# A value product in eleven passes instead of twelve, with the low half of the probabilities written in two pieces

## The chip, the cores and the metric

The kernel runs on one core of one Trainium2 chip. The metric is the device time of one execution in microseconds; the median of three runs of the kernel before is 1019.92 us (1019.78 to 1021.08). The engines are named as in the profile: PE (TensorE matmuls), PEld (weight loads), DVE (VectorE), ACT (ScalarE), POOL (GpSimd) and SP (the engine whose queue issues most of the DMAs).

## The reference

Attention over 8 batches and 12 heads of 448 tokens and 64 channels, followed by a gated feed-forward stage with token mixing:

```python
q_n, k_n = rmsnorm(q, g_q), rmsnorm(k, g_k)
attn = softmax(q_n @ k_n.T / sqrt(64))
x = attn @ v                               # back to (8, 448, 768)
x_prev = x shifted by one token
xk = mu_k * x + (1 - mu_k) * x_prev        # xr likewise with mu_r
k = relu(xk @ w_k)                         # 768 -> 1024
out = sigmoid(xr @ w_r) * ((k * k) @ w_v)  # 1024 -> 768
```

## The kernel before

**Number format.** Inputs are f32, and PE multiplies f16. An f32 value is therefore held as a sum hi + lo of two f16 numbers, and a product of two such values is made of three f16 products: hi·hi, hi·lo and lo·hi. The first batch (quads 0 to 2, pairs 0 to 5) is done in f32 instead.

**Tiling of the attention.** Two heads are a pair (48 pairs, six to a batch) and two pairs a quad (24 quads). The keys of a head are 448 = 3.5 chunks of 128. `scores` makes, for 128 queries and both heads of a pair, two score tiles `sc` of 128x448 in PSUM; there are seven such groups in a quad. `expo` takes the row maximum (DVE) and the exponential (ACT). `probs` computes the reciprocal of the row sum, and `split` writes the normalized probabilities into a tile `nat` of the ring of that name (a borrowed buffer of it is called `natx` in the trace): ACT writes hi as f16, then one DVE instruction writes lo = value − hi, 448 wide. When both heads are split, one DMA transpose on SP's queue turns `nat` into the tile `pT`, so that keys lie on partitions. From quad 3 on there are 21 quads x 7 groups x 2 heads = 294 such splits.

**Value product.** `attends` multiplies, for each pair, `pT` by the values (`vh` and `vl`, hi and lo f16). Flat in `nat` stand hi of head 0, hi of head 1, lo of head 0, lo of head 1, so 14 chunks of 128. Chunk 3 is half head 0 and half head 1, and the value layout prepared on the host has zeros in the half that is not meant. The product takes 4 chunks of hi by `vh` and by `vl`, and 4 chunks of lo by `vh`: the 12 passes of `PASSES`. A pass is two matmuls, one for each head, side by side in the two column halves of the array; each streams 448 columns. The result goes into the PSUM tile `ot`, and ACT copies it into an `x` tile.

**Feed-forward.** For each batch, `mix` blends x and x_prev into `xk` (for `w_k`) and `xr` (for `w_r`): POOL, then DVE (the instruction that writes `df` or `dfx`), then ACT (hi) and POOL (lo). `moe` then runs on PE: the key product of a batch (`mm<-xk,wkh` in the trace, 144 matmuls), which needs all six `xk`, and then the output products (`mm<-wrh,xr` and `mm<-wvh,kk`, 252 or 336 matmuls). The weights too are scaled and split on the chip during the first batches; the first output product waits for the last weight tile.

**Order.** A planner (`Plan`) runs when the kernel is built. Every step above is a thread that yields instructions; the planner keeps a clock for each engine, prices each instruction (`price`) and repeatedly emits the one that could start first, less a priority. The order it finds is fixed for each engine, and an engine runs its instructions in that order: one that waits holds back all that stands behind it. For a DVE instruction of n elements with two tensor inputs the price is n/0.96 + 128 ns above 64 elements, and n/0.96 + 64 ns up to 64. Priorities put the `xk` mixes forward while `moe` wants them; the feed-forward matmuls fill PE between the attention's steps.

Of the kernel before, what the change touches and what calls it, by code (L numbers as in the profile page):

```python
# [12 lines left out]
AF = mybir.ActivationFunctionType  # L13
ALU = mybir.AluOpType
# [3 lines left out]
HD = 64  # L18
NT = 7
S = NT * HD  # L20
# [57 lines left out]
U32 = 3  # L78
# [42 lines left out]
def whole(ap):  # L121
    c = ap.shape[-1]
    return ap.rearrange("p a c -> p (a c)").bitcast(F32).rearrange("p (a c) -> p a c", c=c)
# [297 lines left out]
def attn_moe_kernel(tc, q, k, v, g_q, g_k, mu_k, mu_r, w_k, w_v, w_r, out):  # L421
# [13 lines left out]
    T, V, A, G_, SP = (Engine(n, e) for n, e in (("PE", nc.tensor), ("DVE", nc.vector), ("ACT", nc.scalar), ("POOL", nc.gpsimd), ("SP", nc.sync)))  # L435
# [23 lines left out]
    NQ, NPAIR, NSS, NSL = len(quads), len(pairs), 4 * NT, (NT + 1) // 2  # L459
# [10 lines left out]
    def until(f):  # L470
        while not f():
            yield f
# [33 lines left out]
    for name, plan_ in (("kk", KK_LENT), ("xk", XK_LENT)):  # L506
# [4 lines left out]
        o = 0  # L511
        for n in plan_:
            r = R[n]
# [172 lines left out]
    def vfree(i, vf):  # L686
        FR[i] = FR.get(i, 0) + 1
        if FR[i] == 2:
            VFREE.append(vf)
# [66 lines left out]
    def scores():  # L756
        for gi, (u, x, t0) in enumerate(groups):
# [31 lines left out]
            for j in range(2):  # L789
                plan.spawn(expo(gi, j, both, sums, D, tp), PRIO_E)  # L790
            plan.spawn(probs(gi, both, sums, D, tp), PRIO_E)

    def expo(gi, j, both, sums, D, tp):
# [11 lines left out]
    def probs(gi, both, sums, D, tp):  # L805
        u, x, t0 = groups[gi]
        yield from until(lambda: len(D) == 2 and st["g"] == gi)
        for i in (2 * u, 2 * u + 1) if t0 == NT - 1 else (2 * u + x,):
            if i not in PT:
                yield from until(lambda: PTFREE[i % 2] and (i != 2 * U32 or PTFREE[1]))  # L810
                PTFREE[i % 2] = False
                PT[i] = (whole(PTQ[:, :, :]) if u < U32 else PTQ)[:, :, i % 2 * S:(i % 2 + 1) * S]
                CNT[i] = 0
        if tp is not None:
            st["g"] += 1
            yield from probs_pe(u, x, t0, sums, tp)
            return
        tp = yield from R["nat"].get(u < 3)
        ph = tp.rearrange("p a c -> p (a c)").rearrange("p (a c) -> p a c", c=S)
        st["g"] += 1  # L820
        r = sums[:, 8:11:2]
        yield V.tensor_scalar(out=r, in0=both[0][:, S:S + 2], scalar1=1e-9, scalar2=2.0 ** -15, op0=ALU.add, op1=ALU.mult)
        yield V.reciprocal(out=r, in_=r)
        E = {}
        for j in range(2):
            plan.spawn(split(j, both[j], r, ph, E), PRIO_P)
        yield from until(lambda: len(E) == 2)
        phf = ph.rearrange("p a c -> p (a c)")
        if t0 < NT - 1:
            yield SP.dma_start_transpose(out=PT[2 * u + x][:, :, (t0 + x) * HD:(t0 + x + 2) * HD], in_=phf)  # L830
            CNT[2 * u + x] += 1
        else:
            yield SP.dma_start_transpose(out=PTQ[:, :, S - HD:S + HD], in_=phf)
            CNT[2 * u] += 1
            CNT[2 * u + 1] += 1
        R["nat"].put(tp)

    def probs_pe(u, x, t0, sums, tp):
        r = sums[:, 8:11:2]
        yield V.tensor_scalar(out=r, in0=sums[:, 4:7:2], scalar1=1e-9, scalar2=2.0 ** -15, op0=ALU.add, op1=ALU.mult)  # L840
        yield V.reciprocal(out=r, in_=r)
        tf = tp.bitcast(F32).rearrange("p a c -> p (a c)")
        for j in range(2):
            w = tf[:, j * S:(j + 1) * S]
            yield G_.tensor_scalar(out=w, in0=w, scalar1=r[:, j:j + 1], scalar2=0.0, op0=ALU.mult, op1=ALU.add)
        c0 = S - HD if t0 == NT - 1 else x * S + (t0 + x) * HD
        for a0 in range(0, NT, 4):
            m = min(4, NT - a0)
            st["zq"] += 1
            z = yield from banks["sc"].get()  # L850
            st["zq"] -= 1
            yield [T.transpose(form=("tr", TR_COST * m), out=z[:, a * P:(a + 1) * P], in_=tf[:, (a0 + a) * P:(a0 + a + 1) * P], identity=ident) for a in range(m)]
            src = z[:, 0:m * P].rearrange("p (a c) -> p a c", c=P)
            if u < U32:
                dst = whole(PTQ[:, :, :])[:, a0:a0 + m, c0:c0 + P]
                yield A.copy(out=dst, in_=src) if plan.pick("ACT", "DVE") == "ACT" else V.tensor_copy(out=dst, in_=src)
            else:
                hi, lo = (PTQ[:, h + a0:h + a0 + m, c0:c0 + P] for h in (0, NT))
                yield A.copy(out=hi, in_=src)
                yield V.tensor_tensor(out=lo, in0=src, in1=hi, op=ALU.subtract)  # L860
            banks["sc"].put(z)
        R["nat"].put(tp)
        for i in (2 * u, 2 * u + 1) if t0 == NT - 1 else (2 * u + x,):
            CNT[i] += 1

    def split(j, sp, r, ph, E):
        yield A.activation(out=ph[:, j], in_=sp[:, 0:S], func=AF.Copy, scale=r[:, j:j + 1])
        yield V.scalar_tensor_tensor(out=ph[:, 2 + j], in0=sp[:, 0:S], scalar=r[:, j:j + 1], in1=ph[:, j], op0=ALU.mult, op1=ALU.subtract)
        E[j] = True
        banks["sc"].put(sp)  # L870

    PASSES = [p for c in range(NSL) for p in ((0, 0, c), (0, 1, c))] + [(1, 0, c) for c in range(NSL)]

    def attends():
        for i in range(NPAIR):
            yield from until(lambda: CNT.get(i) == 4 and i in VV)
            x = yield from R["x"].get()
            vh, vl, iv = VV.pop(i)
            pT = PT.pop(i)
            av = yield from banks["ot"].get()  # L880
            ops = []
            passes = [(0, 0, c) for c in range(NSL)] if vl is None else PASSES
            for j, (pl, hl, c) in enumerate(passes):
                for h in range(2):
                    ops.append(T.matmul(
                        form=("av", len(passes) * (4 if vl is None else 1) * S / 2.368),
                        out=av[h * HD:(h + 1) * HD, 0:S],
                        lhsT=(vl if hl else vh)[:, NSL * h + c, :],
                        rhs=pT[:, NT * pl + (NSL - 1) * h + c, :],
                        start=(j == 0), stop=(j == len(passes) - 1)))  # L890
            yield ops
            PTFREE[i % 2] = True
            if vl is None:
                vfree(i, vh)
            else:
                R["vh"].put(vh)
                R["vl"].put(vl)
            for lo, hi in ((0, NT),) if i % 2 == 0 else ((NT - 1, NT), (0, NT - 1)):
                o = 0 if i % 2 == 0 or lo else HD
                yield A.activation(out=x[:, 1 + lo:1 + hi, :].rearrange("p t c -> p (t c)"), in_=av[:, o:o + (hi - lo) * HD], func=AF.Copy, scale=1.0 if iv is None else iv)  # L900
            banks["ot"].put(av)
            yield G_.memset(out=x[:, 0, 0:1], value=0.0)
            yield G_.tensor_copy(out=x[:, 0, 1:HD], in_=x[:, NT, 0:HD - 1])
            XT[i] = [x, 2]
# [247 lines left out]
def layouts(inputs):  # L1152
    import numpy as np

    q, k, v = (np.asarray(inputs[n]) for n in ("q", "k", "v"))
    b, h = q.shape[:2]
    nq = b * h // 4

    def tokens(a):
        return a.reshape(b, h, HD, NT, HD)  # L1160

    def quads(a):
        a = tokens(a).reshape(nq, 2, 2, HD, NT, HD)
        return np.ascontiguousarray(a.transpose(0, 1, 3, 2, 4, 5)).reshape(nq, P, 2 * S)

    qd, kd = quads(q), quads(k)
    a = tokens(q).reshape(nq, 4, HD, NT, HD)[PE_T:]
    pair = a[:, :, :, :NT - 1].reshape(-1, 4, HD, NT // 2, 2, HD).transpose(0, 4, 2, 3, 1, 5).reshape(-1, P, (NT - 1) * 2 * HD)
    last = a[:, :, :, NT - 1].reshape(-1, 2, 2, HD, HD).transpose(0, 1, 3, 2, 4).reshape(-1, P, 2 * HD)
    qd[PE_T:] = np.concatenate([pair, last], axis=2)  # L1170
    a = tokens(v).reshape(b * h // 2, 2, HD, NT, HD)
    n = (NT + 1) // 2
    vd = np.zeros((b * h // 2, 2, HD, 2 * n, HD), v.dtype)
    for x in range(2):
        for e in range(2):
            t = (x + e) % 2
            o = n * x + (x and not e)
            c = (NT + 1 - t) // 2
            vd[:, e, :, o:o + c] = a[:, x, :, t::2]
    return {"q": qd, "k": kd, "v": vd.reshape(b * h // 2, P, 2 * n * HD)}  # L1180


# [30 lines left out]
```

## Time and profile before

| | |
|---|---|
| median of three runs | 1019.92 us |
| the profiled execution | 1018.41 us, of which its span is 1016.6 us |
| busy over the span | PE 923.4 us (91%), DVE 790.2 (78%), ACT 744.7 (73%), POOL 691.1 (68%) |
| matmuls of the value product, pairs 6 to 47 | 672 with `vh`, 336 with `vl` |
| DVE instructions that write lo of the probabilities | 244 into `nat` and 50 into `natx`, mean 674 ns |

PE's share of 91% is an average over a start in which it waits and a long stretch in which it hardly does, so the stages have to be read apart. The granted clock of PE is 0.97 on average; it is lower only in the first 235 us and in the last two.

### The profile page before, as it was taken

Reading aid. Unit: us, or ns where it says so; the run is one execution under the profiler, and the core shown is the slowest. Engines: PE = TensorE matmul, PEld = TensorE weight load, DVE = VectorE, ACT = ScalarE, POOL = GpSimd, SP = SyncE. Lnnn points to the kernel's source line nnn. Section 1 sums busy time; section 2 is a strip of 40 time slices with the busy share of each in tenths; the row PEclk is TensorE's granted clock in tenths of the full one; section 3 lists DMA queues with packets and bytes.
Section 4 is the critical chain, followed back from the end, with each engine's and each line's share of the span. In section 5 each row is a group of like instructions: output and inputs, shape, how many; then the busy total and the mean of one; then the engine's idle time right before and its main releaser. Section 6 shows DMA issues by size and latency. Waiting matters only on the chain. (4 is left out here: it accounts for less than half of the span.)

```text
span 1016.6 us, 18482 instructions
## 1 busy us (share of the span) xinstructions
PE 923.4 (91%) x6166; PEld 486.1 (48%) x6166; DVE 790.2 (78%) x1969; ACT 744.7 (73%) x1753; POOL 691.1 (68%) x734
## 2 busy tenths in 40 slices
PE   1577868859999999999999999999998999999998
PEld 1343434434544555445544555455444554455564
DVE  5797979978999798979996898799887998753000
ACT  3576858978698889888987888988896898842311
POOL 2687879841789577968787659965886567556501
PEclk9798969978999999999999999999999999999999
DMA  7323358776794998698858968877877897440000
GB/s 244 111 91 89 103 150 167 168 180 120 179 189 106 203 203 183 144 191 191 174 131 170 195 144 198 186 155 163 173 139 168 195 188 163 103 78 32 1 33 31
DMA packets 371134, 148.14 MB, mean 146 GB/s; under 512 B 338272, under 2 KB 355168, under 8 KB 371040
## 3 DMA queue, kind: packets, MB, share of 16 engines
q1 hardware_dynamic: 351792, 129.20, 57.9%
q10 hardware_dynamic: 19248, 17.77, 5.9%
q8 instruction: 48, 0.79, 0.3%
q14 instruction: 46, 0.38, 0.1%
HBM read 51.98 MB, written 11.01 MB: 62 GB/s over the span
## 5 line engine op out<-in xcount | busy, mean ns | idle before, releaser
L272 PE MATMUL mm<-wvh,kk 128*128 128x384 f16 x896 | 234.1, 326 | 3.4 <-POOL kk L272 3.0
L272 ACT ACTIVATE sc<-sc,sums 128x448 f32<-128x448 f32 x294 | 181.3, 620 | 41.7 <-DVE sums L272 38.5
L272 PE MATMUL mm<-xk,wkh 128*128 128x448 f16 x768 | 208.3, 353 | 3.7 <-DVE bstat L272 1.8
L272 DVE TENSOR_REDUCE sums<-sc 128x1 f32<-128x448 f32 x336 | 193.0, 612 | 11.6 <-PE sc L272 11.0
L272 ACT ACTIVATE nat<-sc,sums 128x448 f16<-128x448 f32 (+1 forms) x274 | 166.8, 652 | 20.9 <-DVE sums L272 7.2
L272 PE MATMUL mm<-wrh,xr 128*128 128x384 f16 x672 | 177.3, 328 | 0.0
L272 PEld LDWEIGHTS <-kk 128*128 128x128 f16 (+1 forms) x1362 | 129.6, 98 | 99.5 <-issue 14.9
L272 DVE SCALAR_TENSOR_TENSOR nat<-sc,sums,nat 128x448 f16<-128x448 f32 x244 | 159.6, 674 | 19.9 <-ACT nat L272 19.3
L272 PE MATMUL mm<-wvl,kk 128*128 128x384 f16 x448 | 146.0, 326 | 0.0
L272 PE MATMUL sc<-stk 64*128 64x448 f16 (+3 forms) x1104 | 129.1, 378 | 11.7 <-DVE nat L272 7.8
L272 PE MATMUL mm<-xk,wkl 128*128 128x448 f16 x384 | 135.3, 352 | 0.0
L272 PEld LDWEIGHTS <-xr 128*128 128x128 f16 x1008 | 96.1, 98 | 72.5 <-issue 12.5
L272 PE MATMUL mm<-wrl,xr 128*128 128x384 f16 x336 | 110.0, 327 | 0.0
L272 PEld LDWEIGHTS <-wkh 128*128 128x128 f16 x768 | 72.0, 98 | 78.6 <-issue 17.4
L272 PE MATMUL ot<-pT,vh 128*64 128x448 f16 x672 | 100.9, 359 | 5.4 <-DMA pT<-nat 5.4
L272 DVE SCALAR_TENSOR_TENSOR o<-o,mm 128x384 f32<-128x384 f32 x56 | 30.5, 545 | 90.4 <-PE mm L272 60.1
L272 POOL TENSOR_TENSOR qk<-qk,ss 128x896 f32<-128x896 f32 x36 | 62.9, 1749 | 42.6 <-DVE ss L272 19.2
L272 POOL TENSOR_TENSOR o<-o,bsc 128x384 f32<-128x384 f32 x48 | 42.8, 891 | 61.0 <-DVE o L272 48.7
L272 ACT ACTIVATE o<-mm,bsc 128x128 f32<-128x128 f32 x144 | 44.3, 386 | 49.5 <-PE mm L272 37.4
L272 DVE SCALAR_TENSOR_TENSOR df<-x,bsc,df 128x448 f32<-128x448 f32 x68 | 66.5, 993 | 4.2 <-POOL df L272 4.0
L272 POOL TENSOR_TENSOR nat<-qk,nat 128x896 f16<-128x896 f32 x29 | 56.3, 1940 | 19.3 <-ACT nat L272 19.1
L272 POOL TENSOR_TENSOR nat<-nat 128x448 f32<-128x448 f32 x38 | 45.0, 1184 | 34.8 <-ACT nat L272 15.8
(166 smaller groups left out, 1782.2 us busy)
## 6 DMA issues: line engine op xcount, KB each, us to landing
vf<-in_v_dram SPq DMA_DIRECT2D x48, 256.0 KB, 3.1
out_dram<-o SPq DMA_DIRECT2D x28, 384.0 KB, 2.8
qk<-in_k_dram SPq DMA_DIRECT2D x23, 448.0 KB, 4.4
qk<-in_q_dram SPq DMA_DIRECT2D x22, 448.0 KB, 4.2
raw<-in_moe_w_v_dram ACTq DMA_DIRECT2D x12, 512.0 KB, 4.5
raw<-in_moe_w_r_dram ACTq DMA_DIRECT2D x12, 384.0 KB, 3.3
kk<-in_moe_w_k_dram ACTq DMA_DIRECT2D x8, 384.0 KB, 3.9
raw<-in_moe_w_k_dram ACTq DMA_DIRECT2D x8, 384.0 KB, 4.1
```

The lines of the kernel that those rows point to most:

```text
L272: r = op.fn(op.kw["out"], op.kw["value"]) if op.fn.__name__ == "memset" else op.fn(**op.kw)
```

## The change

Within `nat` the halves now stand by head: hi and lo of head 0 (896 columns, seven chunks), then hi and lo of head 1. Lo is written in rotated order: its last 64 columns come first, right behind hi. Chunk 3 of a head is then the last 64 keys of hi followed by the last 64 keys of lo, and chunks 4 to 6 are the rest of lo. The host's value layout holds the last 64 keys twice, once for each half of that chunk. So one pass by `vh` does the half chunk of hi and that of lo together; the pass by `vl` over the same chunk adds a lo·lo term. Passes for a pair: chunks 0 to 3 by `vh` and `vl`, and chunks 4 to 6 by `vh`, 11 instead of 12. Because of the rotation the DVE instruction that wrote 448 columns of lo becomes two, of 64 and of 384 columns. The f32 pairs (`PASSES32`) keep their layout. Number and size of the DMAs stay as they were.

```diff
     def split(j, sp, r, ph, E):
-        yield A.activation(out=ph[:, j], in_=sp[:, 0:S], func=AF.Copy, scale=r[:, j:j + 1])
-        yield V.scalar_tensor_tensor(out=ph[:, 2 + j], in0=sp[:, 0:S], scalar=r[:, j:j + 1], in1=ph[:, j], op0=ALU.mult, op1=ALU.subtract)
+        yield A.activation(out=ph[:, j, 0:S], in_=sp[:, 0:S], func=AF.Copy, scale=r[:, j:j + 1])
+        for a, n, o in ((S - HD, HD, S), (0, S - HD, S + HD)):
+            yield V.scalar_tensor_tensor(out=ph[:, j, o:o + n], in0=sp[:, a:a + n], scalar=r[:, j:j + 1], in1=ph[:, j, a:a + n], op0=ALU.mult, op1=ALU.subtract)
...
-    PASSES = [p for c in range(NSL) for p in ((0, 0, c), (0, 1, c))] + [(1, 0, c) for c in range(NSL)]
+    PASSES = [(c, l, c) for c in range(NSL) for l in range(2)] + [(NSL + c, 0, c) for c in range(NSL - 1)]
+    PASSES32 = [(c, 0, c) for c in range(NSL)]
...
-                        rhs=pT[:, NT * pl + (NSL - 1) * h + c, :],
+                        rhs=pT[:, (NSL - 1 if vl is None else NT) * h + pc, :],
...
+            k = slice(2 * U32, None)
+            vd[k, e, :, n * x:n * x + n] = a[k, x][:, :, [e + 2 * m if m < n - 1 else NT - 1 for m in range(n)]]
```

Since durations and matmul counts enter the planner, the order on every engine also changes from the first split on. Two places matter below.

On DVE, the first place is where the last mix for batch 3's key product stands (the instruction that writes `dfx`). Before:

```order
L272 TENSOR_SCALAR sums_107<-sc_5846 128x2
L272 RECIPROCAL sums_107<-sums_107 128x2
L272 TENSOR_REDUCE vs<-ot_5921 128x1
L272 SCALAR_TENSOR_TENSOR dfx_5942<-x_5753,bsc,dfx_5942 128x448
L272 TENSOR_SCALAR sums_108<-sc_5896 128x2
L272 SCALAR_TENSOR_TENSOR o_5803<-o_5803,mm_5842 128x384
```

And the same mix in the changed kernel:

```order
L272 RECIPROCAL sums_109<-sums_109 128x2
L272 TENSOR_REDUCE sums_110<-sc_6091 128x1
L272 SCALAR_TENSOR_TENSOR nat_6047<-sc_5949,sums_108,nat_6047 128x64
L272 SCALAR_TENSOR_TENSOR nat_6047<-sc_5949,sums_108,nat_6047 128x384
L272 SCALAR_TENSOR_TENSOR dfx_6021<-x_5850,bsc,dfx_6021 128x448
L272 SCALAR_TENSOR_TENSOR nat_6115<-sc_6056,sums_109,nat_6115 128x64
L272 SCALAR_TENSOR_TENSOR nat_6115<-sc_6056,sums_109,nat_6115 128x384
```

Each lo now stands as two rows. 134 splits stand ahead of this mix where 130 stood; at the last mix for batch 5 it is 216 in both kernels, so there the attention's share of DVE's work is the same and only the second pieces are more.

On PE, the second place is just ahead of the value product of pair 9 (`ot<-pT,vh`). Before, batch 0's first output products (`mm<-wrh,xr`) stand there:

```order
L272 MATMUL mm_2540<-wrh,xr_1610 128x384
L272 LDWEIGHTS xr_1610
L272 MATMUL mm_2540<-wrl,xr_1610 128x384
L272 LDWEIGHTS xr_1610
L272 MATMUL mm_2540<-wrh,xr_1610 128x384
L272 LDWEIGHTS vh_2122
L272 MATMUL ot_2446<-pT,vh_2122 64x448
```

In the changed kernel scores (`sc<-stk`) stand there, and the output products begin only behind this value product:

```order
L272 MATMUL sc_2436<-stk_2109 128x448
L272 LDWEIGHTS stk_2109
L272 MATMUL sc_2437<-stk_2109 128x448
L272 LDWEIGHTS stk_2109
L272 MATMUL sc_2436<-stk_2109 128x448
L272 LDWEIGHTS vh_2089
L272 MATMUL ot_2455<-pT,vh_2089 64x448
```

Before, 192 feed-forward matmuls stand ahead of pair 9's value product, now 144. At the end of the program 594 stood behind the last value product, now 582.

More of the change, by code (lines that the diff above doesn't have):

```diff
@@ L818, in probs @@
         tp = yield from R["nat"].get(u < 3)
-        ph = tp.rearrange("p a c -> p (a c)").rearrange("p (a c) -> p a c", c=S)
+        ph = tp.rearrange("p (h a) c -> p h (a c)", h=2)
         st["g"] += 1
@@ L827, in probs @@
         yield from until(lambda: len(E) == 2)
-        phf = ph.rearrange("p a c -> p (a c)")
+        phf = tp.rearrange("p a c -> p (a c)")
         if t0 < NT - 1:
@@ L881, in attends @@
             ops = []
-            passes = [(0, 0, c) for c in range(NSL)] if vl is None else PASSES
-            for j, (pl, hl, c) in enumerate(passes):
+            passes = PASSES32 if vl is None else PASSES
+            for j, (pc, hl, c) in enumerate(passes):
                 for h in range(2):
```

## The prediction, made before the changed kernel ran

> **What bounds the kernel now.** I read busy time by stage first, cut where PE stops waiting (235 us), at two starts of a key product (502.9 and 717.7) and at the end of the attention (911).
>
> ```profile
> core 0: us, PE busy (x) PEld busy (x) DVE busy (x) ACT busy (x) POOL busy (x), PEclk, DMA share, GB/s
> 153.00:235.00 82.00, 61.88 (x418) 31.12 (x415) 72.03 (x172) 68.24 (x149) 55.01 (x61) 0.90 0.75 163
> 235.00:502.90 267.90, 266.34 (x1862) 138.29 (x1861) 237.52 (x590) 225.79 (x542) 198.34 (x197) 1.00 0.80 172
> 502.90:717.70 214.80, 212.24 (x1472) 109.44 (x1471) 188.09 (x462) 182.07 (x434) 161.16 (x160) 1.00 0.79 172
> 717.70:911.00 193.30, 187.35 (x1301) 96.62 (x1299) 158.16 (x376) 152.21 (x365) 132.89 (x141) 1.00 0.71 151
> 911.00:1016.60 105.60, 100.81 (x598) 58.04 (x594) 14.30 (x21) 23.70 (x58) 37.94 (x42) 1.00 0.06 23
> ```
>
> From 153 to 235 us DVE is busy 88% and PE 75%: the vector engines lead. From 235 to 717.7 PE is idle 4.1 us of 482.7, and DVE 57.1. The last 105 us are feed-forward on PE alone. So PE binds after 235, with DVE 88% full beside it. The waits say how near the two are, first PE's from 235 to 787, then DVE's longest from 235 to 717.7:
>
> ```profile
> PE sc L272 <- DVE nat L272: 5.1, 7, 1.9
> PE mm L272 <- POOL kk L272: 3.0, 2, 2.1
> ...
> DVE nat L272 <- ACT nat L272: 11.1, 23, 1.2
> DVE sums L272 <- ACT sc L272: 8.1, 14, 1.3
> DVE sst L272 <- POOL nat L272: 7.3, 7, 2.2
> ```
>
> Where PE waits at all it is for the lo that DVE writes. DVE's own waits are short and on ACT and POOL, not on PE: DVE isn't idle because PE holds it back, so its 57 us are only partly room. Next, how far ahead of PE the mixes are. A key product needs the last lo of `xk` (POOL):
>
> ```profile
> 717.51 1.04 POOL L272 TENSOR_TENSOR xk<-dfx,xk 128x448 f16<-128x448 f32 x1
> 717.68 0.54 PE L272 MATMUL mm<-xk,wkh 128*128 128x448 f16 x2
> 718.06 0.35 PE L272 MATMUL mm<-xk,wkl 128*128 128x448 f16 x1
> ...
> 914.39 1.03 POOL L272 TENSOR_TENSOR xk<-dfx,xk 128x448 f16<-128x448 f32 x1 [1.40 <-ACT xk L272]
> 929.81 0.35 PE L272 MATMUL mm<-xk,wkh 128*128 128x448 f16 x1
> ```
>
> Batch 5's product starts at 717.68 while its last operand is done at 718.55. That operand is the sixth of six chunks; with three matmuls to a chunk at 0.19 us (two from 717.68 to 718.06) it is read 15 matmuls or 2.9 us after the start if it is the last in order, 2.3 if it is the fifth. The margin is between 1.4 and 2.0 us; I take 1.6. Batch 7 has 929.81 − 915.42 = 14.4 us. A delay of the vector engines therefore shows at batch 5 first.
>
> **Removed: one pass for each of 42 pairs.** The value product from 235 us on, and one of them in the chain of work:
>
> ```profile
> L272 PE MATMUL ot<-pT,vh 128*64 128x448 f16 x624 | 92.5, 356 | 0.0
> L272 PE MATMUL ot<-pT,vl 128*64 128x448 f16 x312 | 55.5, 352 | 0.0
> ...
> 882.28 2.39 PE ot L272 x24
> ```
>
> 936 matmuls are 39 pairs of 24. One pair takes 2.39 us, so a pass (two matmuls) takes 2.39/12 = 0.199 us. 39 x 0.199 = 7.8 us fall where PE binds; three pairs lie earlier, where PE waits anyway, and I count nothing for them. The weight loads that go run beside matmuls: nothing.
>
> **Added: 294 DVE instructions.** The trace has no 64-wide one of this form (PSUM source, pointer scalar, f16 out). Its neighbours:
>
> ```profile
> L272 DVE SCALAR_TENSOR_TENSOR nat<-sc,sums,nat 128x448 f16<-128x448 f32 x244 | 159.6, 674 | 19.9 <-ACT nat L272 19.3
> L272 DVE SCALAR_TENSOR_TENSOR stk<-sc,gc,stk 128x512 f16<-128x512 f32 x3 | 2.2, 743 | 0.1
> L272 DVE SCALAR_TENSOR_TENSOR stk<-sc,gc,stk 128x384 f16<-128x384 f32 x3 | 1.8, 606 | 0.0
> L272 DVE TENSOR_TENSOR stk<-sc,stk 128x512 f16<-128x512 f32 x3 | 2.0, 681 | 3.6 <-ACT stk L272 3.6
> L272 DVE TENSOR_TENSOR stk<-sc,stk 128x384 f16<-128x384 f32 x3 | 1.6, 545 | 0.0
> L272 DVE TENSOR_TENSOR gk<-gq,ident 64x64 f32<-64x64 f32 x2 | 0.4, 214 | 0.0
> ...
> 801.75 0.67 DVE L272 SCALAR_TENSOR_TENSOR nat<-sc,sums,nat 128x448 f16<-128x448 f32 x1
> 802.34 0.17 DVE L272 TENSOR_TENSOR stm<-sst,ss 128x28 f32<-128x28 f32 x1
> ```
>
> The 384-wide piece is in the table: 606 ns. Without the pointer scalar 384 takes 545 and 64 takes 214, 1.03 ns an element down to 64; the scalar adds 62 at 512 and 61 at 384, so I take 214 + 61 = 275, or 606 − 320 x 1.07 = 264 along the other line: 272 ns. In a row of instructions the next one starts 0.08 us before the end (801.75 + 0.67 against 802.34). So a split costs DVE 526 + 192 instead of 594: **+124 ns**. The bounds: 66 ns if the 64-wide one costs 134 (214 − 80, no scalar), 204 ns if nothing overlaps. The planner's own price, 131 for 64 columns, makes it 64; so the order is planned for half of what I expect. Over 294 splits it is 36 us (19 to 60). By stage:
>
> ```profile
> L272 DVE SCALAR_TENSOR_TENSOR nat<-sc,sums,nat 128x448 f16<-128x448 f32 x28 | 18.5, 672 | 2.8 <-ACT nat L272 2.8
> ...
> L272 DVE SCALAR_TENSOR_TENSOR nat<-sc,sums,nat 128x448 f16<-128x448 f32 x155 | 101.1, 674 | 11.6 <-ACT nat L272 11.1
> L272 DVE SCALAR_TENSOR_TENSOR natx<-sc,sums,natx 128x448 f16<-128x448 f32 x38 | 25.3, 674 | 4.3 <-ACT natx L272 4.3
> ```
>
> *153 to 235 us:* 28 x 0.124 = 3.5 us. Here the vector engines lead, and the last weight tile, for which batch 0's output products wait, comes behind these splits (26 of them now, 25 before). I take all of it: +3.5. The ends are 0, and 8, the 48 output matmuls (0.163 us each) that no longer stand ahead of pair 9.
>
> *235 to 717.7 us:* 193 x 0.124 = 23.9 us on an engine with 57 us of idle time. How much reaches PE depends on how many splits stand on the chain that sets the time. The chain by line and the splits in the same window, first 744.6 to 817.5 (72.9 us), then 744.6 to 911 (166.4 us):
>
> ```profile
> by line: PE mm L272 13.8%; DVE sums L272 13.8%; issue 13.4%; DVE nat L272 9.0%; DMA pT<-nat 6.9%; DVE bsc L272 5.8%; ACT nat L272 3.9%; PE sc L272 3.8%; ACT sc L272 3.5%; DVE stm L272 3.3%; ACT vh L272 2.7%; DVE ss L272 2.6%; ACT o L272 2.0
> L272 DVE SCALAR_TENSOR_TENSOR nat<-sc,sums,nat 128x448 f16<-128x448 f32 x30 | 19.8, 674 | 3.5 <-ACT nat L272 3.5
> L272 DVE SCALAR_TENSOR_TENSOR natx<-sc,sums,natx 128x448 f16<-128x448 f32 x2 | 1.4, 675 | 0.0
> ...
> by line: PE mm L272 47.2%; PE ot L272 8.7%; PE sc L272 8.1%; DVE sums L272 6.0%; issue 5.9%; DVE nat L272 4.0%; DMA pT<-nat 3.0%; DVE bsc L272 2.5%; ACT nat L272 1.7%; ACT sc L272 1.5%; DVE stm L272 1.4%; ACT vh L272 1.2%; DVE ss L272 1.2%;
> L272 DVE SCALAR_TENSOR_TENSOR nat<-sc,sums,nat 128x448 f16<-128x448 f32 x54 | 35.6, 674 | 5.5 <-ACT nat L272 5.4
> L272 DVE SCALAR_TENSOR_TENSOR natx<-sc,sums,natx 128x448 f16<-128x448 f32 x12 | 7.8, 674 | 0.6 <-ACT natx L272 0.6
> ```
>
> 9.0% of 72.9 us is 6.6, 11 splits at 0.59, of 32 that ran: a share of 0.35. Over 166.4 us it is 11 of 66, 0.17. Before 744 PE waits even less, so I take 0.22, nearer the second: 23.9 x 0.22 = 5.3 us; less the margin of 1.6, batch 5's product starts 3.7 us later than 717.7 (and the early 3.5 on top). The ends are −5.4 (nothing comes through, and the mixes come forward with PE) and 22.3 (all). As the mixes then set that start, the 27 pairs ahead of it pay nothing: PE, 27 x 0.199 = 5.4 us sooner there, waits 3.7 + 5.4 = 9.1 us. Only the passes behind it pay: pairs 36 to 47, 12 x 0.199 = 2.4 us. Behind 717.7 batch 7's margin of 14.4 us covers what is added (78 splits, 9.7 us). SP's queue gets the same transposes, each behind a lo that ends later; ACT and POOL get nothing.
>
> **Sum.** 1018.4 (the profiled execution, 1.8 beside its span) + 3.5 + 3.7 − 2.4 = 1023.2. The median of the runs lies 1.5 above that execution, so 1024.7; I say 1024.5. Against 1019.9 that is 0.45% slower; 0.2% (2 us) is about what can be told from no change.
>
> **Rivals.** (a) *PE binds as before.* DVE's idle time takes all that is added, and the mixes come forward with PE. For it: PE idle 4 us of 483, and some forty short waits on DVE that could shrink. Against it: at batch 5 the mixes must come 5.4 − 1.6 = 3.8 us earlier than now with more work ahead of them. 1018.4 + 3.5 − 7.8 + 1.5 = 1015.6; 1011.5 if nothing is lost early and all 42 passes pay (8.4). It decides for faster where, without the early loss, less than 2 of the 23.9 us come through. (b) *Loss and gain cancel,* 1018 to 1022: by the sum above a share from 0 (1019.4) to 0.1 (1021.8). (c) *DVE becomes the bound,* every lo on the chain: 1019.9 + 3.5 + 22.3 − 2.4 = 1043; DVE would have to run without a gap, as it does in no stage of the table but for short stretches. (d) *The wait comes in one piece and takes PE's clock with it.* The trace has one such case:
>
> ```profile
> 217.52 0.59 PE L272 MATMUL ot<-pT,vh 128*64 128x448 f16 x2 [5.42 <-DMA pT<-nat]
> ...
> 215.00:223.00 8.00, 5.43 (x34) 2.87 (x34) 3.52 (x5) 3.31 (x8) 2.33 (x4) 0.62 0.76 213
> 223.00:235.00 12.00, 7.07 (x36) 3.34 (x37) 11.15 (x31) 9.53 (x22) 2.28 (x2) 0.72 0.25 40
> ```
>
> Behind a wait of 5.4 us the clock is 0.62 for 8 us and 0.72 for 12, 0.38 x 8 + 0.28 x 12 = 6.4 us of PE lost; the waits of at most 2.1 us after 235 leave it at 1.00. A single wait of 9 us at batch 5 would thus give 1024.5 + 6.4 = 1031; my forecast has it in pieces, at batches 3 and 5 and at scores. The Trainium skill ("TensorE: Matmul & The Clock Gate", Part 1) states the rule: after an idle window of about 3.4 us the array runs at half clock until it has been busy as long. The trace agrees: no drop behind 2.1 us, a drop behind 5.4.
>
> **Chances.** The forecast, with a share of 0.12 to 0.5, 1022 to 1031: 0.31. (d), 1028 to 1036: 0.12. (c) 0.06. Together slower: 0.49. (b), the same: 0.22. (a), faster: 0.29. The range leaves out (c) and a little of (a) and (d): 1011.5 to 1035; the forecast's own is 1022 to 1031.
>
> **What would show it.** A value product of 22 matmuls in 2.19 us: right on the pass. The new DVE rows at 264 to 275 and 606 ns: right on the price; near 214, half of it. DVE busy 815 to 830 us instead of 790. PE idle between 235 and 720 us of 8 us or more, with waits on `xk` or on `nat` at batches 3 and 5: right on the way it goes. If PE's idle time there stays at 4 us, rival (a) holds and I am wrong; if PE's full stretch begins at 235 us again instead of 3.5 us later, the early term is wrong.

## The result, and the profile after

The changed kernel takes 1026.41 us (median of five, 1025.33 to 1029.21), the kernel before 1019.92 on the same chip. The ratio is 1.0064 with a 95% interval of 1.0047 to 1.0081: slower by 0.64%, 6.5 us. The forecast was 1024.5. The profiled execution took 1026.64 us, 8.2 us more than the one of before. What follows looks at where these microseconds are, and then whether they came by the way that was forecast. In large part they did not.

Busy time by stage in the changed kernel, columns as in the same view of before:

```profile
153.00:235.00 82.00, 60.40 (x408) 29.64 (x406) 80.03 (x208) 69.30 (x151) 55.70 (x64) 0.92 0.75 168
235.00:502.90 267.90, 262.71 (x1802) 135.61 (x1799) 236.55 (x677) 219.28 (x521) 188.03 (x188) 0.99 0.78 164
502.90:717.70 214.80, 205.75 (x1414) 103.85 (x1412) 195.78 (x534) 179.11 (x427) 158.72 (x160) 1.00 0.77 170
717.70:911.00 193.30, 188.33 (x1290) 96.12 (x1289) 169.73 (x473) 160.14 (x379) 140.55 (x142) 1.00 0.71 155
911.00:1024.50 113.50, 108.68 (x653) 62.62 (x651) 17.79 (x31) 27.06 (x67) 40.68 (x47) 0.99 0.10 33
```

PE's idle time from 235 to 717.7 us is 5.2 + 9.1 = 14.2 us where it was 4.1. What PE waits for from 235 to 911 us (total, times, longest):

```profile
PE sc L272 <- DVE nat L272: 8.9, 10, 1.6
PE sc L272 <- DMA stk<-nat: 4.8, 2, 2.5
PE sc L272 <- DVE natx L272: 2.3, 4, 1.1
```

All three are waits of a score product: for a PSUM bank that DVE's lo still reads, or for transposed q and k. No wait on `xk` appears. The two costs that could be priced beforehand, first the groups of DVE instructions that write lo, then one value product in the chain:

```profile
L272 DVE SCALAR_TENSOR_TENSOR nat<-sc,sums,nat 128x384 f16<-128x384 f32 x256 | 154.8, 605 | 0.1
L272 DVE SCALAR_TENSOR_TENSOR nat<-sc,sums,nat 128x64 f16<-128x64 f32 x256 | 69.9, 273 | 16.4 <-ACT nat L272 15.7
```

```profile
876.82 2.20 PE ot L272 x22
```

They measure 605 and 273 ns (606 and 272 were taken) and 2.20 us for 22 matmuls (2.19). DVE's busy time is 819.2 us, 29 more. So the ingredients are as expected. The best cut through the whole run is by landmarks on PE: the first output product of batch 0, and the starts of the key products of batches 1 and 7. In the kernel before and in the changed one:

```profile
232.35 0.50 PE L272 MATMUL mm<-wrh,xr 128*128 128x384 f16 x1
289.81 0.54 PE L272 MATMUL mm<-xk,wkh 128*128 128x448 f16 x2
```

```profile
239.71 0.34 PE L272 MATMUL mm<-wrh,xr 128*128 128x384 f16 x1
296.99 0.54 PE L272 MATMUL mm<-xk,wkh 128*128 128x448 f16 x2
937.68 0.54 PE L272 MATMUL mm<-xk,wkh 128*128 128x448 f16 x2
```

Before, batch 7 started at 929.81. From batch 1 to batch 7 it took 640.0 us and now takes 640.7, so by these landmarks 7.2 of the 7.9 us lie ahead of batch 1. The two stretches don't hold the same work, however. PE's matmuls that read `vh` between the two starts (us, busy, count, then the clock), before and in the changed kernel:

```profile
289.81:929.81 640.00, 85.36 (x576) 1.00 0.75 162
296.99:937.68 640.69, 76.64 (x490) 1.00 0.73 158
```

A pair has 16 such matmuls before and 14 now, so 576 are 36 pairs and 490 are 35. The new order has moved one value product ahead of batch 1, and with it six score matmuls (816 are left between the starts, where 822 were). At 2.20 and 0.67 us, the length of such a product and of six scores in the changed kernel's chain, that is 2.9 us of work that has only changed places. About 4.3 of the 7.9 us are then lost ahead of batch 1 and 3.6 behind it, where 35 pairs' shorter products do not pay for the added DVE work. The experiments ask whether the loss belongs to the added work or to the new order, and what the pass and the pieces are worth by themselves.

### The profile page after: what moved, and what is told of

It reads as the page before. It is cut to its first block, busy times and chain, and to the rows that moved or that the text cites. A ratio compares the mean times of both kernels' runs of the same rounds, so it can differ in the third digit from the quotient of the medians.

```text
span 1024.5 us, 18629 instructions
## 1 busy us (share of the span) xinstructions
PE 921.4 (90%) x6082; PEld 481.3 (47%) x6082; DVE 819.2 (80%) x2263; ACT 747.4 (73%) x1753; POOL 690.4 (67%) x734
## 5 line engine op out<-in xcount | busy, mean ns | idle before, releaser
L272 DVE SCALAR_TENSOR_TENSOR nat<-sc,sums,nat 128x64 f16<-128x64 f32 (+1 forms) x512 | 202.3, 439 | 16.5 <-ACT nat L272 15.7
L272 ACT ACTIVATE nat<-sc,sums 128x448 f16<-128x448 f32 (+1 forms) x286 | 174.0, 654 | 24.4 <-DVE sums L272 11.8
L272 PE MATMUL sc<-stk 64*128 64x448 f16 (+3 forms) x1104 | 131.3, 380 | 25.7 <-DVE nat L272 10.6
L272 PE MATMUL ot<-pT,vh 128*64 128x448 f16 x588 | 94.7, 366 | 4.9 <-DMA pT<-nat 3.9
L272 DVE SCALAR_TENSOR_TENSOR df<-x,bsc,df 128x448 f32<-128x448 f32 x68 | 70.8, 1051 | 4.9 <-POOL df L272 4.7
L272 PEld LDWEIGHTS <-stk 64*128 64x128 f16 x1008 | 33.7, 97 | 85.7 <-DVE nat L272 25.0
```

What stands on the lines that cost most here:

```text
L272: r = op.fn(op.kw["out"], op.kw["value"]) if op.fn.__name__ == "memset" else op.fn(**op.kw)
```

## Experiments: the order held fixed

Two theories stood at the start. *Load:* each split costs DVE 124 ns more, part of it reaches PE, and PE's relief is not usable where the vector engines set the pace. *Order:* the new prices led the planner to another order, and that costs. They can be told apart because the planner can be made to produce either order for either code: it is given the other kernel's prices, while the instructions stay. All instructions but the ones changed then stand in the same order on every engine. Every kernel was timed in five rounds beside the kernel before.

**New code, old order.** The planner is told the old prices, and the two pieces are one step of it:

```diff
-        for a, n, o in ((S - HD, HD, S), (0, S - HD, S + HD)):
-            yield V.scalar_tensor_tensor(...)
+        ops = []
+        for a, n, o in ((S - HD, HD, S), (0, S - HD, S + HD)):
+            ops.append(V.scalar_tensor_tensor(...))
+        ops[0].as_width = S          # priced as one of 448 columns
+        yield ops
...
-                        form=("av", len(passes) * (4 if vl is None else 1) * S / 2.368),
+                        form=("av", (16 if vl is None else 12) * S / 2.368),
```

> The changed kernel's instructions (11 passes, lo in two pieces), with every engine's order as in the kernel before: the planner is told the old prices (12 passes, one lo of 448 columns), and the two pieces stand side by side. Theory 1 (load: each split costs DVE 124 ns more, part of it reaches PE, and PE's shorter products cannot be used where the mixes set the start): slower than before also in this order, 1022 to 1032, PE idle between 235 and 718 us 10 us or more, DVE busy 815 to 825. Rival 2 (order: the new prices made the planner find a worse order, and the load itself is hidden): 1011 to 1018, since the old order then keeps the gain of 7.8 us.

Measured: 1037.11 us, ratio 1.0162 (1.0138 to 1.0186). Load holds, at more than its upper bound. The order rival falls in this form: in the old order the changed code is slower still.

**Old code, new order.** One lo of 448 columns, emitted at the second of two planner steps priced as 64 and 384; the value product priced as 11 passes and run as 12.

> The instructions of the kernel before (12 passes, one lo of 448 columns), with every engine's order as in the changed kernel: the planner is told the new prices. Theory 1 (load): within 4 us of before, 1016 to 1024. Rival 2 (order): 1024 to 1034, as slow as the changed kernel or slower, since the passes are 8 us more.

Measured: 1027.05 us, ratio 1.0061 (1.0040 to 1.0082). So the new order alone costs as much as the whole change. Both theories were half right, and the effects do not add: 1.62% and 0.61% apart, 0.64% together.

**The pass alone, old order.** 11 passes; lo in one instruction, unrotated.

```diff
+        yield V.scalar_tensor_tensor(out=ph[:, j, S:2 * S], in0=sp[:, 0:S], scalar=r[:, j:j + 1], in1=ph[:, j, 0:S], op0=ALU.mult, op1=ALU.subtract)
```

> Only the pass is saved: 11 passes, lo in one instruction of 448 columns, order of the kernel before. Lo's columns stay unrotated, so in the passes over lo they meet the values of other keys. Theory 1: PE's relief alone is 42 x 0.199 = 8.4 us, but the mixes that start batches 3 and 5 are only 0 to 2 us ahead, so between 1.6 and 7.8 us come through: 1012 to 1018. Rival 2 (order): the full 7.8, 1012. Rival 3 (the pass saves nothing, since the time is set by the vector engines throughout): 1019 to 1020.

Measured: 1020.25 us, ratio 0.9999 (0.9979 to 1.0019). In this order no gain of the 42 passes can be seen, and by the interval it is 2 us at most; rival 3 comes true. Batches 1 and 7 start here:

```profile
294.31 0.54 PE L277 MATMUL mm<-xk,wkh 128*128 128x448 f16 x2
933.01 0.54 PE L277 MATMUL mm<-xk,wkh 128*128 128x448 f16 x2
```

638.7 us from one to the other, 1.3 less than before, where 36 passes take 7.2 us on PE. PE is idle for 14.8 us of this stretch where it was for 10.1, so most of what it saved it waited for. The first cause is the same as before, but 9.6 us of it for 5.6 (235 to 911 us):

```profile
PE sc L277 <- DVE nat L277: 9.6, 14, 2.1
```

**The pieces alone, old order.** 12 passes, lo in 64 + 384 columns, priced as one.

> Only the two pieces: 12 passes, lo in 64 + 384 columns, order of the kernel before. DVE busy +29 us as in the changed kernel. Theory 1: 1024 to 1034, PE waits between 235 and 718 us for DVE's lo and for what comes after it. Rival 2 (order): 1019 to 1022, DVE's idle time takes the 36 us.

Measured: 1037.06 us, ratio 1.0163 (1.0135 to 1.0190). The 294 added instructions cost 16.8 us, the same as the changed code in this order. The waits of PE and the two starts:

```profile
PE sc L277 <- DVE nat L277: 13.6, 17, 2.0
```

```profile
294.10 0.54 PE L277 MATMUL mm<-xk,wkh 128*128 128x448 f16 x2
949.56 0.54 PE L277 MATMUL mm<-xk,wkh 128*128 128x448 f16 x2
```

655.5 us, 15.5 more than before. 248 of the 294 splits stand behind batch 1's mixes; at 124 ns they are 30.8 us, so half of what DVE does more arrives at the end of the program. Of the 15.5 us, 10.3 are idle time of PE, and 3.4 are two drops of its clock behind waits (last section).

**The pass alone and the pieces alone, new order.** The same two codes as above, with the prices of the changed kernel.

> 11 passes and one lo of 448 columns, order of the changed kernel. Lo's columns stay unrotated, so in the passes over lo they meet the values of other keys. So far: old code in the new order 1027, pass only in the old order 1020 (nothing gained). Theory 1 (in any order the vector engines set the pace and the pass saves nothing): 1025 to 1028. Rival 2 (the new order moved the limit to PE, so there the pass pays): 1018 to 1021.

> 12 passes and lo in two pieces, order of the changed kernel. Theory 1 (each split's 124 ns come through by the same half as in the old order, where they made 16.8 us): 1036 to 1044, and the changed kernel's 1026 would then be a gain of 10 or more from the pass. Rival 2 (the new order is planned for the two pieces and hides most of them; PE's passes bind): 1030 to 1035. Rival 3 (neither matters in this order): 1025 to 1029.

Measured: the pass alone 1017.17 us, ratio 0.9967 (0.9950 to 0.9983); the pieces alone 1030.95 us, ratio 1.0099 (1.0079 to 1.0119). Rival 2 holds in both. The starts of batches 1 and 7, first with the pass alone, then with the pieces alone:

```profile
296.93 0.54 PE L277 MATMUL mm<-xk,wkh 128*128 128x448 f16 x2
928.54 0.54 PE L277 MATMUL mm<-xk,wkh 128*128 128x448 f16 x2
```

```profile
297.40 0.54 PE L272 MATMUL mm<-xk,wkh 128*128 128x448 f16 x2
942.04 0.54 PE L272 MATMUL mm<-xk,wkh 128*128 128x448 f16 x2
```

With the old code in the new order they are at 300.25 and 940.81. All eight cases side by side (batches 1 to 7 from the one profiled execution of each, in us, and how much of that PE is idle):

| code | old order: ratio | batches 1 to 7 | PE idle | new order: ratio | batches 1 to 7 | PE idle |
|---|---|---|---|---|---|---|
| old | 1 | 640.0 | 10.1 | 1.0061 | 640.6 | 9.6 |
| pass alone | 0.9999 | 638.7 | 14.8 | 0.9967 | 631.6 | 11.1 |
| pieces alone | 1.0163 | 655.5 | 20.4 | 1.0099 | 644.6 | 15.5 |
| both | 1.0162 | 652.7 | 25.4 | 1.0064 | 640.7 | 17.5 |

The table is to be read within one order: in the new one the stretch holds a pair and six scores less, some 3 us, in all four kernels.

In the old order the pass gives 1.3 to 2.8 us from batch 1 to 7 and the pieces cost 14 to 15.5: the vector engines set the pace. In the new order the pass gives 9.0 with the old lo and 3.9 with the new one, and the pieces cost 4.1 with twelve passes and 9.1 with eleven. That looks as if whichever engine is relieved, the other were next, but PE's idle time says it more simply, for within an order it adds up. The pass adds 4.7 to 5.0 us of waiting in the old order, of 7.2 saved, and 1.5 to 2.0 in the new one, of 7.0. The pieces add 10.3 to 10.6 us in the old order and 5.9 to 6.4 in the new one. So the new order hides more of both.

In these traces the uneven gains in the new order come from PE's clock. With the old code there, PE waits three times for a transpose, 3.2, 2.0 and 2.1 us, and its granted clock is 0.83 over the 10 us around each of these waits (columns as in the stage views):

```profile
336.00:346.00 10.00, 6.76 (x37) 3.03 (x36) 6.73 (x21) 6.46 (x15) 7.98 (x10) 0.83 0.90 199
667.00:677.00 10.00, 7.62 (x41) 3.65 (x40) 8.04 (x26) 8.76 (x23) 6.79 (x8) 0.83 0.92 203
766.00:776.00 10.00, 7.87 (x52) 3.65 (x52) 5.56 (x16) 7.49 (x18) 8.65 (x9) 0.83 1.06 212
```

That is 1.7 us each time, 5.1 in all. The pass alone has no such drop in this order, the two kernels with pieces have one each, and the old code in the old order has none. The waits from batch 1 to 7 are no longer in total than in the old order (9.6 us for 10.1); so in this trace, the slowest of seven runs, what the new order costs the old code in that stretch is clock and not waiting. The seven runs have a mean granted clock of 0.965 and the 18 of the kernel before beside them 0.968, which fits, but no trace shows the drops of the other runs.

Batch 1 starts at 297 to 300 in all four kernels of the new order and at 290 to 294 in the four of the old one, 5 us apart on average. The value product and the scores that stand ahead of it make 3 of the 5, and the other 2 are less than what the four kernels of one order differ by among themselves. PE's idle time ahead of batch 1 is 78.3 us before, 80.8 in the changed kernel and 77.4 with the old code in the new order. That the 48 output matmuls moved behind pair 9 cost anything is not shown.

## Experiments: is a wrong price behind the order, or chance?

The planner prices the 64-wide piece at 131 ns, its measured pace is 273 − 80 = 193. If that error is what spoils the order, the right price mends it.

```diff
-        c = n / 0.96 + (128 if two and n > 64 else 64)
+        c = n / 0.96 + (128 if two and (n > 64 or hasattr(kw.get("scalar"), "tensor")) else 64)
```

> The changed kernel, with one number of the planner changed: a DVE instruction with two tensor inputs and a pointer scalar is priced with 128 ns beside its elements at any width, so the piece of 64 columns at 195 ns instead of 131 (measured 273 less an overlap of 80). Theory (the order is planned for half of the cost, and engines drift from it): 1018 to 1023. Rival (any new order is as good or bad as another, some us either way): 1023 to 1031.

Measured: 1019.57 us, ratio 0.9989 (0.9974 to 1.0003), 0.75% better than the changed kernel, and just as the theory wanted it. Two more prices tell whether it is the reason:

> The changed kernel with only the planner's price of the 64-wide piece changed, to 163 ns, half way between the 131 of the changed kernel (ratio 1.0064) and the 195 measured (0.9989). Theory 1 (the error of the price is what costs): in between, ratio 1.000 to 1.005. Rival (each order is a draw, the price only shakes it): anything from 0.995 to 1.012, with no trend over 131, 163, 195, 259.

> The same with 259 ns, 64 above the measured pace. Theory 1: not better than at 195, ratio 0.999 to 1.005. Rival (draw): anything from 0.995 to 1.012.

Measured: at 163 ns 1033.67 us, ratio 1.0130 (1.0106 to 1.0155); at 259 ns 1042.91 us, ratio 1.0216 (1.0194 to 1.0237). By price, 131, 163, 195, 259: 1.0064, 1.0130, 0.9989, 1.0216. There is no trend. Half way to the right price the kernel is worse than without correction, and both theories' bounds for 163 and 259 are broken on the upper side. With the old order's 1.0162 this makes five orders of the same instructions over a span of 2.3%. The theory of the price falls by the run at 163. That the order is a draw is what remains, not something that four prices with one order each can prove: without 163 they would still fit a best price near the right one. What the four orders differ in can be seen: PE's idle time from 235 to 911 us is, by price, 19.2, 23.4, 12.5 and 28.0 us, and the times follow it. In the worst of them, at 259, PE waits up to 4.3 us at a time, and its clock suffers as well, from 717.7 to 911 us:

```profile
717.70:911.00 193.30, 183.02 (x1242) 91.50 (x1241) 168.22 (x466) 157.18 (x373) 138.51 (x143) 0.96 0.73 158
```

## Experiments: giving DVE room

**Less work on DVE, old code, old order.** The 147 instructions that add 1e-9 to the row sums and scale them are left out.

```diff
-        yield V.tensor_scalar(out=r, in0=both[0][:, S:S + 2], scalar1=1e-9, scalar2=2.0 ** -15, op0=ALU.add, op1=ALU.mult)
-        yield V.reciprocal(out=r, in_=r)
+        yield V.reciprocal(out=r, in_=both[0][:, S:S + 2])
...
-        yield V.tensor_scalar(out=sc[:, 2:4], in0=ismu, scalar1=sc[:, 0:1], scalar2=2.0 ** -15, op0=ALU.mult, op1=ALU.mult)
+        yield V.tensor_scalar(out=sc[:, 2:4], in0=ismu, scalar1=sc[:, 0:1], scalar2=1.0 if b else 2.0 ** -15, op0=ALU.mult, op1=ALU.mult)
```

> The kernel before in its own order, with less work on DVE: the instruction that adds 1e-9 to the row sums and scales them (147 times, 150 ns, some 70 where it overlaps) is left out from batch 1 on, and the reciprocal reads the sums from PSUM; the factor 2^15 is left out of the probabilities and restored behind. DVE busy 8 to 12 us less. Theory 1 (in this order DVE's work sets the pace, and about half of it comes through): 1014 to 1017. Rival (the pace is set by waits among the engines that do not depend on DVE's amount of work, so adding hurts but taking away does not help): 1019 to 1021.

Measured: 1019.14 us, ratio 0.9976 (0.9957 to 0.9995); DVE busy 780.1 us, 10 less. About a quarter of the 10 us comes through (0.5 to 4.4 us by the interval), between theory and rival. Taking away seems to help less than adding hurts, where it was a half; but the interval nearly reaches that.

**The same, planned anew, in the old code and in the new code (with the price of 195).**

> The kernel before without the 147 small DVE instructions on the row sums (the reciprocal reads the sums from PSUM; the factor 2^15 is left out of the probabilities from batch 1 on and restored behind), planned anew. In the old order this gave 0.9976. Theory 1 (DVE and PE limit together; once DVE has room, PE's passes are what is left): 0.993 to 0.998. Rival (draw): 0.994 to 1.008.

> The changed kernel with both: the 64-wide piece priced at 195 ns and the 147 small DVE instructions left out (the factor 2^15 as in the run beside it). Theory 1: DVE's added 36 us are cut by 10, so more of the 8.4 us of passes come through than at 0.9989: 0.991 to 0.997, and faster than the old code with fewer DVE instructions. Rival (the pass is worth nothing even then): not faster than that run.

Measured: old code 1015.48 us, ratio 0.9951 (0.9934 to 0.9967); new code 1017.56 us, ratio 0.9966 (0.9944 to 0.9988). Both beat the kernel before and the changed kernel. The two cannot be told apart by these intervals, and with a draw of the order in each, they do not settle whether the pass pays once DVE has room. The version to keep is the old code with fewer DVE instructions; in it the probabilities lack the factor 2^15, which should cost their lo halves accuracy; no run here measures how much.

## Why the prediction came out right, and which steps were wrong

- **Price of the pass and of the pieces:** right, to 1%. Taking the pointer scalar's 61 ns over to the 64-wide form, from rows of 384 and 512, held: 273 ns. DVE's busy time rose by 29 us rather than the 36 of the sum. With the order held, the pieces alone raise it by 32. In the changed kernel other rows are shorter, most of all the 16 small instructions `bsc<-mu,bsc`, 5.2 us for 11.2; why was not followed up.
- **The early term (+3.5 us, all to the load):** not borne out as a cost of the load. By the sign that was named for it, it looks right: PE is busy 0.79 us of the four up to 235 and all of the four behind, where before it was 3.88 of the four up to 235, so its full stretch begins some 3.5 us later. But with the pass alone in the old order, which has no added load, PE is busy 1.55 us of the four up to 235 as well, at a clock of 0.70 and then 0.50. Batch 1's start moved by 7.2 us, of which 2.9 are work that the new order put ahead of it. The rest is within what the start varies by between kernels of one order, and the old code in the new order starts batch 1 later still. What the sum left out is the order's own effect.
- **The share of 0.22 (+5.3 us up to batch 5):** mis-sized for a fixed order, where it is 0.5. The chain of waits showed 0.17 to 0.35, and only from 744.6 us on. In the new order some 239 second pieces, 29.6 us, lie between batches 1 and 7; 4.1 to 9.1 us of that come through, and as idle time of PE 5.9 to 6.4, or 0.20 to 0.22. That is the value taken, but the trace it was read from had the other order, where PE's idle time alone makes 0.34: that it fits is luck.
- **"The mixes set the start of batch 5":** the step that failed in kind. The changed kernel has no wait on `xk` from 235 to 911 us; PE waits at score products. The vector engines' pace reaches PE there in many small waits (17 of at most 2.0 us in the kernel with the pieces alone, old order), not at one barrier. The rows read for the prediction had them: 5.1 us at scores, beside 3.0 for `kk` of POOL, which its reading passed over. PE's idle time from 235 to 717.7 us rose by 10.1 us; 9.1 was forecast, but from a wait at that start.
- **"The 27 passes ahead of batch 5 pay nothing":** right in the old order, where not even the later ones pay, and wrong in the new one, where the pass gives 3.9 to 9.0 us and PE waits for only 1.5 to 2.0 of the 7.0 saved.
- **Rivals:** (a), that PE binds and the passes pay, is true in its half about the passes, for the pass alone in the new order. (d) did not come as one wait at batch 5. In small it did: one drop of 1.7 us in the changed kernel, three with the old code in the new order, and the clock of 0.96 above at a price of 259. Its 6.4 us were counted over 20 us in which PE is busy for 12.5.
- **The sum:** −2.4, +3.7 and +3.5 came out at +4.8 us, and +6.5 was measured. By the table one can go two ways: the new order first, +6.2, and then pass and pieces, +0.3; or pass and pieces in the old order first, +16.5, and then the new order, −10. Neither is the sum of the forecast. The total was near because errors cancelled, and the sign rested on an order that nothing in the profile of before could show: with the price of 195 the same code is no slower than before. So the number was luck in good part.

## What to carry to other kernels

Where a planner or scheduler makes the order, a change of code is two changes: new work, and a new order. Hold the order fixed by giving the planner the old prices, and read the work from that; then try several orders (small changes of a price do) before a difference of 1% is put down to the code or to the planner's accuracy, since one order that confirms a theory proves little.

When one engine is 99% full beside another at 88%, the fuller need not be the one that sets the time. If the other's idle time is made of waits on its neighbours and not on the full one, its idle share is not room: here, with the order held, half of the added work came through, and relief of the full engine gave nothing that could be measured.

Landmarks compare two orders only if the same work lies between them. Count the instructions of each kind on both sides first; here one value product and six scores had crossed a landmark, and an early loss of some 4.3 us looked like 7.2.

## What the hardware showed that was not expected

PE's clock drops after shorter waits than the trace of before let one think, where 2.1 us left it alone. In the changed kernel (a line of the timeline, then the stretch around it):

```profile
337.25 1.30 PE L272 MATMUL sc<-stk 64*128 64x448 f16 x6 [2.29 <-DMA stk<-nat]
```

```profile
336.00:342.00 6.00, 4.75 (x24) 2.06 (x25) 4.97 (x14) 3.87 (x11) 5.80 (x8) 0.72 1.04 230
```

A wait of 2.29 us is followed by a granted clock of 0.72 over 6 us. The length of the wait alone does not decide. First the pieces alone in the old order, where 1.96 us are enough, then the pieces alone in the new order, where 3.52 us leave the clock at 1.00:

```profile
680.55 0.76 PE L277 MATMUL sc<-stk 64*64 64x448 f16 x12 [1.96 <-DVE nat L277]
674.00:688.00 14.00, 11.75 (x83) 5.72 (x82) 12.22 (x47) 12.60 (x33) 2.81 (x6) 0.88 0.36 85
```

```profile
338.67 1.31 PE L272 MATMUL sc<-stk 64*128 64x448 f16 x12 [3.52 <-DMA stk<-nat]
335.00:345.00 10.00, 6.47 (x49) 3.47 (x50) 8.00 (x28) 7.22 (x18) 7.04 (x9) 1.00 0.86 197
```

So the drop can start below the window of about 3.4 us that the Trainium skill gives ("TensorE: Matmul & The Clock Gate", Part 1); its remark that the window runs free of the kernel fits a drop that comes in one case and not in another. The clock records in the 14 traces bear it out. In each trace the changes of the clock lie on one grid of steps of 3.41 us, and a drop to half lasts one or two steps in the stretch from 242 to 1000 us. Each of the 18 drops there begins at the end of a step in which PE was idle for 1.90 us or more; of the 3066 other steps at full clock none has more than 1.94 us of idle time. A wait of 3.5 us that a grid line cuts in half can thus do less harm than one of 2 us within a step.

Also, the start differs from run to run while the instructions are the same: the first 153 us hold no changed instruction (in the kernel before, the first lo is written at 153.6 us), yet the profiled run of the pass alone in the old order reached pair 1's value product at 94.11 us where before it was 91.36. The clock from 30 to 55 us was 0.66 in the one and 0.73 in the other. The kernel before ran between 1016.5 and 1026.1 us in 18 runs beside these experiments; that is why the ratios, and not single times, carry the readings.
